# One more batch turned by a transposing DMA, and a new written order, in a fused attention and channel-mix kernel

## The chip, the core and the metric

The kernel runs on one core of a Trainium2 chip. The engines are named as in the profile: PE multiplies matrices, DVE and ACT work element by element, POOL here issues the loads, and SP issues stores and transposing DMAs. Each engine takes its own instructions strictly in order, and they wait for each other through semaphores. The metric is the device time of one execution in microseconds. A difference of 0.2% (0.4 us) is about what a measurement of this kernel can tell.

## The reference

Inputs are q, k, v of shape 8 x 8 heads x 576 tokens x 64, a scale g of 64, two mixing vectors mu_k and mu_r of 512, and weights w_k (512 x 1024), w_v (1024 x 512), w_r (512 x 512). The reference computes, for each of the eight batches:

```
kv  = k^T v                          # 64 x 64 for each head, over all tokens
u   = q kv
x   = u / sqrt(mean(u*u) + 1e-6) * g # over the 64 of a head; heads side by side: 576 x 512
xk  = mu_k * x + (1 - mu_k) * x_prev # x_prev: x of the token before, zero ahead of the first
xr  = mu_r * x + (1 - mu_r) * x_prev
out = sigmoid(xr w_r) * (relu(xk w_k)^2 w_v)
```

## The kernel before

The kernel keeps x turned (channels on partitions, tokens along the row), in two buffers xT[0] and xT[1] that alternate between batches. The work of a batch goes in stages, each a short function:

- kv (line 282) multiplies k by v; kvo copies the result out of PSUM; from the fifth batch on, kvs (line 299) writes a second copy with the halves of the partitions exchanged.
- q is turned: in the first four batches by PE (qt, line 326, copied out by qto), from the fifth on by a DMA that transposes (qd, line 303).
- u multiplies turned q by kv, in three parts. sq (line 359) squares u on ACT, red (line 363) sums the squares on DVE, and nw (line 367) is eight small DVE instructions that give the inverse root rs. mul (line 397 or 419) multiplies u by rs into y.
- y is turned into xT. There are two ways. In batches one to six PE transposes y into PSUM (x0, line 441, and x, line 450, 36 transposes together) and ACT or DVE copies it into xT multiplied by g (x0o, xo, the helper move on line 427). In batches seven and eight mul writes y into the buffer yd in another order, one DMA on SP transposes all of yd into xT (yd, line 411), and two instructions multiply xT by g in place (gx, line 415). There is one buffer yd, so each batch's mul waits for the DMA of the one before.
- wrap (line 593) fills the first token column, dif (597) takes x minus x_prev, sc (601) multiplies by mu on ACT or DVE, and add (616) adds x_prev: the result is xk (add.b.0) or xr (add.b.1).
- K (line 647) is one 128 x 288 piece of relu(xk w_k): four products on PE and an instruction on ACT or DVE that empties the bank. ks (line 639) squares it into sqk. R (line 654) is 128 tokens of sigmoid(xr w_r). V (line 662) is half of the products with w_v for 128 tokens, and fin (line 678) multiplies V by the sigmoid on DVE and stores it from SP.

The first two batches are cut finer, since their inputs and the weights are still arriving. They have words of their own: for the first batch kvc, qtc, uc, sqc, msc, rsc, mcc (lines 470 to 517; the mean of squares there is a product on PE, msc, and its inverse root on ACT, rsc), Ka and Kz (two halves of a K piece, lines 715 and 719), fu (a fused scale and add on DVE); for the second kvh, uh, sqh, redh, rsh, mulh, xh, x0h and their copies (lines 519 to 585), each for one half of the heads. Kp is a K piece and Vq a quarter of the V products in these batches. wm issues products of zeros that only keep PE busy.

What sets the order is a list written out by hand or by a search, the string ORDER (line 18): eight strings, one a period. The loop on line 795 reads it word by word and issues each word's instructions, so each engine's queue is the list with the other engines' work left out. A word is a name, its arguments (batch from 0, so batch six of this text is 5 in a word), an apostrophe where DVE and not ACT does the element work, and after "=" the PSUM banks to take, of eight. A bank is free again when the instruction that empties it has run. Loads are words as well (ld.0, ld.1, ld.2 for k, v, q), issued from POOL; yd, qd and the stores are issued from SP in the list's order.

```
for word in period.split():
    word, _, digits = word.partition("=")
    chosen[:] = map(int, digits)
    name, *args = word.rstrip("'").split(".")
    ops[name](DVE if word.endswith("'") else ACT, *map(int, args))
```

Of the kernel before, what the change touches and what calls it, by code (L numbers as in the profile page):

```python
# [19 lines left out]
    wm.2.0=1 cast.1' cast.0 kvc.0.2=23 kvco.0' qtc.0.2=45 kvco.1' wm.2.1=6 qtco.0' uc.0=7 qtco.1' uc.1=0  # L20
    qtc.2.2=12 sqc.0 msc.0=3 qtco.2' sqc.1 cols=4 msc.1=6 rsc.0 rsc.1 kvc.2.1=5 kvco.2 uc.2=1 uc.4=4 qtco.3
    mcc.0 mcc.1 difh.0.0.256.576 sc.0.0.0.256.576' sc.0.0.1.256.576' add.0.0.0.256.576 sqc.2 kvc.3.1=3 kvco.3
    msc.2=6 rsc.2 mcc.2 dih.0.2.256.576 fu.0.0.2.256.576 uc.3=5 uc.5=7 sqc.3 sqc.4 wm.2.2=2 msc.3=0 wm.2.4=3
    rsc.3 msc.4=6 mcc.3 dih.0.3.256.576 wrap.0 fu.0.0.3.256.576 wm.2.3=2 sqc.5 msc.5=1 rsc.5 Ka.0.3=3 mcc.5
    wm.1.5=0 rsc.4 mcc.4 Ka.0.2=2 Ka.0.1=5 difh.0.0.0.256 Ka.0.0=1 fu.0.0.0.0.256 Kz.0.3 Kz.0.1 sc.0.1.0
    fu.0.0.1.0.256 difh.0.1.0.256 Kz.0.2 Kz.0.0 Ka.0.7=0 Kz.0.7 fu.0.0.3.0.256 Ka.0.6=6 Kz.0.6 Ka.0.5=7
    fu.0.0.2.0.256 sc.0.1.2 sc.0.1.1' Ka.0.4=4 Kz.0.4' add.0.1.0 Kz.0.5 ksp.0.0.4.8 Kp.0.1.0'=3 Kp.0.1.1=5
    sc.0.1.3 qt.1.0=21 qto.1.0.0' kvh.0=06 kvho.0.1 Kp.0.1.3=4 kvho.0.0' qto.1.0.1' uh.2.0=7 uh.1.0=35 uh.0.0=20
    sqh.0.1.0 ksp.0.1.0.4' sqh.2.0.0 sqh.0.0.0 sqh.1.1.0 sqh.1.0.0 add.0.1.1 Kp.0.1.2=1 ksp.0.0.0.4' Vq.0.2.0=6
    Vq.0.2.1 redh.5.9.0 rsh.5.9.0 redh.0.5.0 rsh.0.5.0 mulh.0.0.0 mulh.0.1.0 Vq.0.1.0=4 Vq.0.1.1 mulh.1.0.0  # L30
    mulh.2.0.0 xh.2.2.0=12 xho.2.2.0.0 xho.2.2.0.1' qt.1.1=03 qto.1.1.0 x0h.0=72 x0ho.0.1' qto.1.1.1 Vq.0.3.0=1
    Vq.0.3.1 x0ho.0.0 kvh.1=20 kvho.1.1 ksp.0.1.4.8' mulh.1.1.0 xh.0.2.0=35 kvho.1.0' uh.2.1=7 uh.0.1=20
    xho.0.2.0.0 sqh.0.0.1 sqh.0.1.1 sqh.2.0.1 ld.0.2 xho.0.2.0.1' ld.1.2 uh.1.1=53 sqh.1.1.1 sqh.1.0.1
    redh.5.9.1 redh.0.5.1 rsh.5.9.1 mulh.0.0.1 Vq.0.1.2 Vq.0.2.2 Vq.0.3.2 rsh.0.5.1 Vq.0.1.3 mulh.1.0.1
    mulh.1.1.1 Vq.0.2.3 Vq.0.0.0=2 mulh.2.0.1 Vq.0.0.1 Vq.0.0.2 mulh.0.1.1 xh.2.2.1=53 xho.2.2.1.0 xh.0.2.1=70
    xho.2.2.1.1' xho.0.2.1.1' ld.2.2 Vq.0.0.3 dif.1.384.576 xho.0.2.1.0 sc.1.0.3.384.576' sc.1.0.1.384.576'
    sc.1.0.2.384.576' sc.1.0.0.384.576' x0h.1=35 x0ho.1.1' x0ho.1.0 wrap.1 adda.1.0.384.576 dif.1.0.384
    sc.1.0.1.0.384' tab R.0.0=0 R.0.1=7 R.0.2=3 fin.0.0
    """,
    """  # L40
    sc.1.1.0 sc.1.0.0.0.384 sc.1.0.3.0.384 fin.0.2 sc.1.0.2.0.384' Kp.1.0.0=5 Kp.1.0.2'=0 add.1.0.0.0.384
    Kp.1.0.3=7 add.1.0.1.0.384 Kp.1.0.1'=3 sc.1.1.2' sc.1.1.3' kv.2=26 Vq.0.3.3 Kp.1.1.2=0 sc.1.1.1' kvo.2.1'
    Kp.1.1.3=5 qt.2.0=73 qto.2.0.0 add.1.1.0 ksp.1.1.2.4 qt.2.1=60 ld.2.3 qto.2.0.1' qto.2.1.1' qto.2.1.0'
    kvo.2.0' Kp.1.1.0=5 Kp.1.1.1'=3 u.2.0=70 ld.1.3 ld.0.3 sq.2.0.0 sq.2.0.1 fin.0.1 Kp.1.1.4=6 add.1.1.1
    R.0.3=2 Kp.1.1.6=5 fin.0.3 u.2.2=3 sq.2.2.0 u.2.1=46 sq.2.1.1 red.2.5.9 sq.2.1.0 R.1.7=2 Kp.1.1.7=5
    red.2.0.5 nw.2.0.1 nw.2.1.2 nw.2.2.3 R.1.6=1 ld.2.4 R.1.5=2 nw.2.3.4 ld.0.4 nw.2.4.5 nw.2.5.6 nw.2.6.7
    nw.2.7.8 ksp.1.1.0.2 R.1.4=5 mul.2.1.0 Kp.1.1.5=1 R.1.8=2 mul.2.2.0 V.1.4.0=4 mul.2.1.1 x0.2=53 mul.2.0.0
    qt.3.1=16 kv.3=27 mul.2.0.1 x0o.2.0 x0o.2.1 ksp.1.0.0.8' x.2.0.4=53 V.1.6.0=0 kvo.3.1 V.1.5.0=7 ksp.1.1.6.8'
    xo.2.0.4.1' wrap.2 ksp.1.1.4.6 V.1.7.0=3 xo.2.0.4.0 dif.2 V.1.7.1 qto.3.1.0' ld.1.4 sc.2.0.1' sc.2.0.3
    sc.2.0.2' sc.2.0.0 add.2.0.1 qto.3.1.1 V.1.4.1 V.1.6.1 add.2.0.0 sc.2.1.2 fin.1.7 V.1.5.1 sc.2.1.0  # L50
    """,
    """
    K.2.3.1=5 sc.2.1.3 sc.2.1.1' K.2.2.0=1 qt.3.0=63 K.2.7.0=5 kvo.3.0' fin.1.6 K.2.6.1=2 K.2.2.1=0 qto.3.0.1'
    ld.2.5 qto.3.0.0' ld.0.5 u.3.0=31 ld.1.5 sq.3.0.1 u.3.2=6 sq.3.0.0 u.3.1=52 qd.4 add.2.1.1 sq.3.2.0 fin.1.5
    fin.1.4 K.2.1.0=0 K.2.3.0=7 add.2.1.0 K.2.0.1'=4 red.3.5.9 sq.3.1.0 sq.3.1.1 red.3.0.5 R.2.3=0 nw.3.0.1
# [12 lines left out]
    K.3.4.0'=7 nw.4.3.4 K.3.2.0=1 nw.4.4.5 nw.4.5.6 ks.3.6' nw.4.6.7 nw.4.7.8 kvs.5.0' ks.3.1 mul.4.2.0
    mul.4.1.1 mul.4.1.0 R.3.8=4 K.3.4.1=7 mul.4.0.0 V.2.3.0=1 R.3.6=4 ks.3.2 ks.3.4 mul.4.0.1 V.2.3.1 R.3.7=7
    x0.4=50 x0o.4.1' x0o.4.0 x.4.0.4=24 u.5.2=6 u.5.0=30 xo.4.0.4.0 sq.5.0.0 u.5.1=75 ld.2.7 ld.0.7 fin.2.3  # L70
    sq.5.0.1 xo.4.0.4.1' ld.1.7 V.3.6.0=1 wrap.4 sq.5.1.0 dif.4 sq.5.1.1 sq.5.2.0 R.3.5=4 V.3.6.1 qd.6 V.3.4.0=2
    sc.4.0.0 red.5.5.9 sc.4.0.1 R.3.4=4 fin.3.6 V.3.4.1 V.3.5.0=1 red.5.0.5 nw.5.0.1 sc.4.0.2 nw.5.1.2 sc.4.0.3
    V.3.5.1 fin.3.4 sc.4.1.0 add.4.0.0 add.4.0.1 nw.5.2.3 nw.5.3.4 V.3.7.0=4 fin.3.5 nw.5.4.5
    """,
    """
    K.4.1.0=2 V.3.7.1 K.4.6.0=1 K.4.5.0=2 nw.5.5.6 sc.4.1.1' nw.5.6.7 fin.3.7 K.4.0.1=4 K.4.0.0=1 sc.4.1.3'
    K.4.5.1=2 K.4.3.1=4 ks.4.0 nw.5.7.8 ks.4.5 mul.5.1.1 mul.5.0.1 K.4.1.1=5 ks.4.1 K.4.2.1=1 mul.5.0.0
    V.3.8.0=0 K.4.7.1=2 add.4.1.0 mul.5.1.0 sc.4.1.2' mul.5.2.0 x0.5=34 x0o.5.0' x.5.0.4=75 xo.5.0.4.0
    xo.5.0.4.1' kv.6=63 kvo.6.0 K.4.4.0=1 kvo.6.1' K.4.7.0=2 K.4.2.0=5 x0o.5.1' ks.4.2 kvs.6.0' kvs.6.1' wrap.5
    dif.5 K.4.3.0=3 K.4.6.1=4 ks.4.7 K.4.4.1=7 add.4.1.1 u.6.2=6 sc.5.0.1' u.6.0=12 sc.5.0.3 ks.4.3' V.3.8.1  # L80
    ks.4.6' ks.4.4 sc.5.0.0' R.4.0=5 sc.5.0.2' V.4.0.0=3 V.4.0.1 add.5.0.1 sq.6.2.0 add.5.0.0 sq.6.0.0 sq.6.0.1
    sc.5.1.3' fin.3.8
    """,
    """
    K.5.4.0=4 u.6.1=75 qd.7 sq.6.1.1 sq.6.1.0 fin.4.0 K.5.5.0=0 K.5.2.1=3 R.4.1=4 K.5.4.1=0 red.6.5.9 red.6.0.5
    nw.6.0.1 nw.6.1.2 nw.6.2.3 R.4.3=3 V.4.1.0=4 nw.6.3.4 nw.6.4.5 nw.6.5.6 nw.6.6.7 nw.6.7.8 mul.6.2.0
    K.5.0.1=0 mul.6.1.1 sc.5.1.2 V.4.3.0=3 V.4.3.1 K.5.6.0=0 K.5.1.0=6 K.5.0.0=5 mul.6.1.0 mul.6.0.1 sc.5.1.1
    kv.7=72 mul.6.0.0 kvo.7.0 sc.5.1.0' K.5.5.1=0 K.5.3.1=1 K.5.6.1'=6 K.5.2.0'=5 add.5.1.0 ks.5.2 kvo.7.1
    K.5.1.1'=7 V.4.1.1 kvs.7.1 kvs.7.0' yd.6 ks.5.1 add.5.1.1 fin.4.1 K.5.7.1=0 fin.4.3 K.5.3.0=1 ks.5.5'
    ks.5.4' K.5.7.0'=6 ks.5.3' u.7.0=52 u.7.2=7 u.7.1=04 ks.5.7' R.5.8=1 sq.7.0.0 R.5.6=3 sq.7.1.1 R.4.2=6  # L90
    gx.6.0' sq.7.0.1 V.4.2.0=1 V.4.2.1 gx.6.1' wrap.6 ks.5.0 dif.6 sq.7.1.0 sc.6.0.2 fin.4.2 R.5.4=3 R.5.5=6
# [28 lines left out]
def kernel(  # L120
# [44 lines left out]
    cols = const.tile([128, 9], FP32, name="cols")  # L165
# [228 lines left out]
    YD = (6, 7)  # L394
    yd = const.tile([128, NHP, 1 + NHP, 128], BF16, name="yd")
# [434 lines left out]
```

## Time and profile before

| what | value |
|---|---|
| median of 3 runs | 199.56 us (199.39 to 199.66) |
| the profiled execution's own time | 199.54 us |
| its span, first to last instruction | 197.8 us |
| PE busy | 188.6 us, 95% of the span |
| DVE busy | 159.3 us, 81% |
| ACT busy | 135.8 us, 69% |
| DMA traffic | HBM read 33.56 MB, written 9.44 MB |

The span is what the profile shows of the program; the execution's own time has a further 1.7 us around it. The page's first part gives each engine's busy time. The chain that ended last is followed back from the last instruction, each step to what released it. A row of the timeline gives the start, the duration of a run of equal instructions, the engine, the line of the code, what is written and read, the count, and in brackets the idle time ahead of it and what ended it. PEld is PE's loading of weights, which runs beside the products.

### The profile page before, as it was taken

To read this page: it belongs to the slowest core of one execution; us is meant where nothing else is said; L and a number is where in the kernel's file an instruction comes from. 1 tells how busy PE (TensorE), PEld (TensorE's weight loads), DVE (VectorE), ACT (ScalarE), POOL (GpSimd) and SP (SyncE) were. 2 spreads that over 40 slices of the span, in tenths; PEclk is the share of its full clock that TensorE was granted. 3 is DMA by queue.
4 is the path that set the end of the run, shared out by engine and by line. 5 is a ranking of instruction groups with operands and counts; after the bars stand their busy time and mean duration, and the time that the engine had idled before them with its cause. 6 is when DMAs were issued, how large, how long until landed. Compare 5 with 4: busy or idle time off the path is not lost.

```text
span 197.8 us, 5867 instructions
## 1 busy us (share of the span) xinstructions
PE 188.6 (95%) x2427; PEld 112.7 (57%) x2451; DVE 159.3 (81%) x348; ACT 135.8 (69%) x284; POOL 26.8 (14%) x44
## 2 busy tenths in 40 slices
PE   7989999999999999999999999999999999999991
PEld 2446844674454756477454775667454754765450
DVE  1499997996999799897999979978999969548240
ACT  3397975968876977979797799766793485637210
POOL 7763342004000400314000000000000000000000
PEclk9999999999999999999999999999999999999999
DMA  5999999999995799999999830559420654021764
GB/s 209 220 206 207 199 207 209 204 227 233 247 213 99 132 209 168 218 247 276 218 209 203 195 74 0 122 116 127 111 55 0 133 124 92 0 53 42 167 132 141
DMA packets 35950, 30.86 MB, mean 156 GB/s; under 512 B 16332, under 2 KB 30932, under 8 KB 35924
## 3 DMA queue, kind: packets, MB, share of 16 engines
q0 software_dynamic: 14912, 16.19, 48.9%
q1 hardware_dynamic: 20612, 13.77, 32.5%
q10 hardware_dynamic: 400, 0.52, 0.9%
q8 instruction: 19, 0.31, 0.6%
q14 instruction: 7, 0.06, 0.1%
HBM read 33.56 MB, written 9.44 MB: 217 GB/s over the span
## 4 chain that ended last, share of the span: by engine, by line
PE 88%; DMA 4%; issue 2%; DVE 2%; POOL 1%; ACT 1%; DVEq 0%; POOLq 0%
PE ps_v L667 29%; PE ps_km L635 29%; PE ps_r L657 16%; DMA rt<-in_v_dram 4%; PE ps_km L712 2%; PE ps_kv L291 2%; PE ps_x L439 2%; PE ps_u L320 2%; PE ps_qt L334 1%; PE ps_u L356 1%; PE ps_v L675 1%; POOL q L184 1%; PE ps_warm L265 1%; ACT sq L549 1%; DVE sqk L643 1%
## 5 line engine op out<-in xcount | busy, mean ns | idle before, releaser
L667 PE MATMUL ps_v<-wv_sb,sqk 128*128 128x512 bf16 x266 | 65.0, 379 | 1.4 <-issue 0.6
L635 PE MATMUL ps_km<-xk,wk_sb 128*128 128x288 bf16 (+3 forms) x480 | 65.0, 285 | 0.0
L635 PEld LDWEIGHTS <-wk_sb 128*128 128x128 bf16 x480 | 45.6, 98 | 16.8
L627 ACT ACTIVATE rt<-ps_km 128x288 bf16<-128x288 f32 (+3 forms) x95 | 39.2, 425 | 22.7 <-PE ps_km L635 19.5
L667 PEld LDWEIGHTS <-sqk 128*128 128x128 bf16 x280 | 26.6, 98 | 29.4 <-DVE sqk L643 0.4
L657 PE MATMUL ps_r<-wr_sb,xr 128*128 128x512 bf16 x136 | 34.9, 379 | 0.6 <-issue 0.2
L680 DVE TENSOR_TENSOR out_sb<-ps_v,sig 128x512 f32<-128x512 f32 (+1 forms) x37 | 24.2, 670 | 8.2 <-issue 3.9
L660 ACT ACTIVATE sig<-ps_r 128x512 bf16<-128x512 f32 x36 | 21.5, 601 | 12.3 <-PE ps_r L657 12.0
L605 ACT ACTIVATE m<-dx,cols 128x576 bf16<-128x576 bf16 (+1 forms) x31 | 22.5, 764 | 2.0 <-DVE dx L599 2.0
L641 ACT ACTIVATE sqk<-rt 128x576 bf16<-128x576 bf16 (+2 forms) x30 | 21.1, 717 | 1.6 <-DVE rt L629 1.5
L657 PEld LDWEIGHTS <-xr 128*128 128x128 bf16 x144 | 13.7, 98 | 14.9 <-issue 0.7
L629 DVE TENSOR_SCALAR rt<-ps_km 128x288 bf16<-128x288 f32 (+3 forms) x25 | 11.8, 477 | 9.9 <-PE ps_km L635 9.7
L365 DVE TENSOR_REDUCE ss<-sq 128x16 f32<-128x1024 bf16 (+1 forms) x12 | 15.9, 1345 | 1.0 <-ACT sq L361 1.0
L361 ACT ACTIVATE sq<-ps_u 128x512 bf16<-128x512 f32 (+1 forms) x30 | 15.2, 565 | 0.6 <-PE ps_u L356 0.3
L643 DVE TENSOR_TENSOR sqk<-rt 128x576 bf16<-128x576 bf16 (+4 forms) x27 | 13.0, 504 | 0.1
L599 DVE TENSOR_TENSOR dx<-xT 128x2304 bf16<-128x2304 bf16 (+5 forms) x13 | 11.6, 895 | 0.9 <-ACT xT L429 0.5
L622 DVE TENSOR_TENSOR xr<-m,xT 128x1152 bf16<-128x1152 bf16 x16 | 11.9, 750 | 0.0
L424 DVE TENSOR_TENSOR y<-ps_u,rs 128x512 bf16<-128x512 f32 (+1 forms) x20 | 11.4, 629 | 0.2
L622 DVE TENSOR_TENSOR xk<-m,xT 128x1152 bf16<-128x1152 bf16 (+2 forms) x16 | 10.8, 699 | 0.9 <-ACT m L605 0.6
L607 DVE TENSOR_SCALAR m<-dx,cols 128x576 bf16<-128x576 bf16 (+3 forms) x35 | 11.2, 351 | 0.1
L265 PE MATMUL ps_warm<-zeros 128*128 128x512 bf16 x22 | 8.4, 517 | 1.5 <-DVE eps L228 1.2
L429 ACT ACTIVATE xT<-ps_x,cols 128x256 bf16<-128x256 bf16 (+3 forms) x13 | 7.0, 563 | 2.9 <-PE ps_x L439 2.9
(91 smaller groups left out, 157.7 us busy)
## 6 DMA issues: line engine op xcount, KB each, us to landing
out_dram<-out_sb SPq DMA_DIRECT2D x67, 128.0 KB, 2.9
sq<-in_k_dram POOLq DMA_DIRECT2D x3, 576.0 KB, 14.5
qT<-in_v_dram POOLq DMA_DIRECT2D x3, 576.0 KB, 14.9
q<-in_q_dram POOLq DMA_DIRECT2D x3, 576.0 KB, 12.8
in_q<-in_q_dram POOLq DMA_DIRECT2D x3, 576.0 KB, 12.6
in_v<-in_v_dram POOLq DMA_DIRECT2D x3, 576.0 KB, 15.7
in_k<-in_k_dram POOLq DMA_DIRECT2D x3, 576.0 KB, 12.6
wk_sb<-in_moe_w_k_dram POOLq DMA_DIRECT2D x2, 512.0 KB, 10.3
```

What stands on the lines that cost most here:

```text
L361: ACT.activation(out=sq[:, rg(t0, n, i) if n else slice(0, 1)], in_=held["u", a, part, i][1], func=AF.Square)
L365: DVE.tensor_reduce(out=ss[:, g0:g1], in_=sq[:, g0:g1], op=ALU.add, axis=AX.X)
L605: eng.activation(out=out_, in_=in_, func=AF.Copy, scale=mu)
L622: DVE.tensor_add(out=dst, in0=m[:, hs, c0:c1], in1=x[:, hs, c0:c1])
L627: eng.activation(out=dst, in_=ps, func=AF.Relu)
L635: nc.tensor.matmul(ps[:, n, :], wk_sb[:, cc, 128 * fc:128 * fc + 128], at[b]["xk"][:, cc, c0:c1], start=(cc == 0), stop=(cc == NHP - 1))
L641: eng.activation(out=sqk[:, fcs, o:o + n], in_=src, func=AF.Square)
L643: eng.tensor_mul(out=sqk[:, fcs, o:o + n], in0=src, in1=src)
L657: nc.tensor.matmul(ps, xr[:, cc, 128 * t:128 * t + 128], wr_sb[:, cc, :], start=(cc == 0), stop=(cc == NHP - 1))
L660: ACT.activation(out=sig[b, t], in_=give("r"), func=AF.Sigmoid)
L667: nc.tensor.matmul(ps, sqk[:, fc, 128 * t:128 * t + 128], wv_sb[:, fc, :], start=(fc == 0), stop=(fc == NFC - 1))
L680: DVE.tensor_mul(out=o, in0=give(key), in1=sig[b, t][:, c])
```

## The change

Batch six (5 in the words) joins the two batches whose y is turned by a DMA: YD grows from (6, 7) to (5, 6, 7). With it x0.5, x.5, x0o.5 and xo.5 leave the list, and yd.5, gx.5.1 and gx.5.0 come into it; mul.5 writes yd instead of y, and mul.5.2.0 becomes two instructions of half the partitions. The eight periods are written anew. All other words stay, at other places: some 65 element words go from ACT to DVE and about as many from DVE to ACT, banks are numbered anew, and words move across the ends of periods. The words that warm PE up go from 12 products ahead of the list and 12 in it (one of them the list's last word) to 12 and 8. In the loads, v and k of batch three change places and k of batch four moves ahead of its q and v.

The first lines of the first period, before and after:

```
-    wm.2.0=1 cast.1' cast.0 kvc.0.2=23 kvco.0' qtc.0.2=45 kvco.1' wm.2.1=6 qtco.0' uc.0=7 qtco.1' uc.1=0
-    qtc.2.2=12 sqc.0 msc.0=3 qtco.2' sqc.1 cols=4 msc.1=6 rsc.0 rsc.1 kvc.2.1=5 kvco.2 uc.2=1 uc.4=4 qtco.3
-    mcc.0 mcc.1 difh.0.0.256.576 sc.0.0.0.256.576' sc.0.0.1.256.576' add.0.0.0.256.576 sqc.2 kvc.3.1=3 kvco.3
...
+    cast.0 cast.1' kvc.0.2=01 kvco.0' kvco.1' qtc.0.2=23 qtco.1' qtco.0 cols=4 wm.1.0=1 uc.1=5 uc.0=6 qtc.2.2=70
+    sqc.1 qtco.2' msc.1=1 sqc.0 msc.0=3 wm.1.1=7 kvc.2.1=4 rsc.0 kvco.2 rsc.1 wm.1.2=7 uc.2=2 qtco.3' uc.4=7
+    sqc.2 wm.1.3=4 kvc.3.1=0 mcc.0 kvco.3 mcc.1 difh.0.0.256.576 msc.2=3 sqc.4 uc.3=4 sc.0.0.0.256.576' uc.5=6
+    sc.0.0.1.256.576' add.0.0.0.256.576 sqc.3 msc.4=1 rsc.2 wm.1.4=0 msc.3=5 wm.3.5=0 Ka.0.0=0 mcc.2 Ka.0.2=3
...
```

Batch two, after (its first half in the first period, its second half in the second):

```
+    ksp.0.1.0.4' sqh.1.1.0 sqh.1.0.0 sqh.0.0.0 add.0.1.1 Kp.0.1.2=5 Kp.0.1.3=6 redh.0.5.0 redh.5.9.0 Vq.0.2.0=1
+    rsh.0.5.0 mulh.2.0.0 mulh.1.1.0 Vq.0.3.0=5 Vq.0.2.1 Vq.0.3.1 x0h.0=62 mulh.1.0.0 sc.0.1.1 qt.1.1=37
+    rsh.5.9.0 mulh.0.0.0 qto.1.1.1 x0ho.0.1' mulh.0.1.0 x0ho.0.0' xh.0.2.0=42 xh.2.2.0=06 xho.0.2.0.1' qto.1.1.0
...
+    sc.1.0.0.0.384 sc.1.1.0 Kp.1.0.1'=6 sc.1.0.2.0.384 Kp.1.0.2=2 Kp.1.0.3'=4 add.1.0.0.0.384 fin.0.2 sc.1.1.1'
+    R.0.0=7 sc.1.0.3.0.384' add.1.0.1.0.384 Kp.1.0.0'=6 R.0.1=4 kv.2=27 kvo.2.0 fin.0.0 Kp.1.1.2=1 sc.1.1.3'
```

Batch six, after (the end of the fourth period and the fifth):

```
+    mul.4.0.1 K.3.4.1=0 x0.4=46 x.4.0.4=73 fin.2.3 x0o.4.0' u.5.1=21 x0o.4.1 u.5.0=50 xo.4.0.4.0 sq.5.1.0
...
+    K.4.5.0=6 mul.5.0.0 mul.5.1.0 mul.5.0.1 kv.6=14 K.4.3.0'=5 K.4.0.1'=6 K.4.6.0=2 yd.5 fin.3.4 sc.4.1.3'
...
+    K.4.2.0=6 K.4.7.0=3 K.4.4.0'=2 ks.4.3' ks.4.1 ks.4.7' gx.5.1' ks.4.4 V.3.8.0=0 u.6.1=51 sq.6.1.0 u.6.2=4
+    gx.5.0' ks.4.2 u.6.0=63 sq.6.0.1 sq.6.1.1 R.4.0=7 wrap.5 sq.6.2.0 V.3.8.1 dif.5 sq.6.0.0 V.4.0.0=2 sc.5.0.2'
...
-    YD = (6, 7)
+    YD = (5, 6, 7)
```

## The prediction, made before the changed kernel ran

> **What bounds the kernel now.** I read the page first: the engines' busy shares and the chain that ended last.
>
> ```profile
> span 197.8 us, 5867 instructions
> ...
> PE 188.6 (95%) x2427; PEld 112.7 (57%) x2451; DVE 159.3 (81%) x348; ACT 135.8 (69%) x284; POOL 26.8 (14%) x44
> ...
> PEclk9999999999999999999999999999999999999999
> ...
> PE 88%; DMA 4%; issue 2%; DVE 2%; POOL 1%; ACT 1%; DVEq 0%; POOLq 0%
> ```
>
> TensorE is busy for 188.6 of 197.8 us, at full clock, and holds 88% of the chain. Next I looked where its idle time lies, stretch by stretch (PE is the first number pair).
>
> ```profile
> 25.00:38.00 13.00, 12.45 (x169) 6.07 (x171) 11.03 (x31) 9.25 (x25) 3.70 (x5) 1.00 1.22 207
> 38.00:48.00 10.00, 9.56 (x220) 6.68 (x220) 8.91 (x21) 7.46 (x15) 2.22 (x3) 1.00 1.19 229
> 48.00:193.00 145.00, 143.79 (x1700) 86.58 (x1715) 121.47 (x251) 102.31 (x212) 6.69 (x9) 1.00 0.74 138
> ```
>
> From 48 to 193 us PE idles 1.21 us in all, in gaps of 0.05 and 0.16 us put down to issue: work that PE loses there shortens the run, and nothing else can gain there. From 25 to 48 us it idles 0.99 us, with DMA loaded throughout. That is the head, where the first two batches wait for inputs and weights. Third, the timeline of the weight loads shows what paces the head:
>
> ```profile
> 15.21 0.12 PEld L712 LDWEIGHTS <-wk_sb 128*128 128x128 bf16 x2 [0.44 <-DMA wk_sb<-in_moe_w_k_dram]
> 17.75 0.52 PEld L712 LDWEIGHTS <-wk_sb 128*128 128x128 bf16 x5 [0.30 <-DMA wk_sb<-in_moe_w_k_dram]
> ```
>
> The two halves of w_k land at 15.2 and 17.7 us, and no order of instructions makes the first products earlier. The same trace has batch two's last part of v landing at 28.85 us; kvh.1, which reads it, starts at 29.17.
>
> **The change part by part.** *Transposes.* The 36 PE transposes of batch six leave:
>
> ```profile
> 114.85 0.63 PE ps_x L439 x36
> ```
>
> The chain of waits gives 0.63 us for them, inside the stretch that PE bounds: −0.63 us. [...]
>
> *Copies.* On DVE two x0o copies (0.28 and 0.27 us) and one xo (0.75) leave, on ACT one xo (1.1). Two in-place products by g come to DVE:
>
> ```profile
> L431 DVE TENSOR_SCALAR xT<-xT,cols x4: 508/512/517, 140.3 to 162.0; 128x1152 bf16<-128x1152 bf16 x4
> L413 SPq DMA_TRANSPOSE xT<-yd x2: 2957/3354/3752, 132.1 to 153.8; - x2
> DMA to landing us min/median/max: 4.9/5.3/5.7
> ```
>
> They are 2 x 0.51 us, and mul.5.2.0 becomes two halves of 0.42 instead of one of 0.41: DVE gains 0.15 us of work, ACT loses 1.1. I count nothing: PE covers it, since the sums below leave DVE slack. Without that cover it would cost 0.15, and it can gain nothing, as PE does not wait for ACT there.
>
> *The new transposing DMA.* yd.5 takes 4.9 to 5.7 us from issue to landing. It waits on SP behind the stores of fin.3.5 and delays those of fin.3.4 and qd.7, whose readers are far off. Behind it on DVE stands gx.5.1', and DVE takes instructions in order, so a late landing holds all that follows: gx.5.0, wrap.5, dif.5, sc, add.5.0, and then PE's K.5. In the new order PE has one kv (0.71 us) and 15 K words (0.49 each) between the last mul of batch six and gx.5.1', 8.06 us; from there 4 V and 4 R halves or tiles (0.86 each) and three u (0.84) to K.5.1.1, 7.75 us. The mul takes 0.68, the DMA 5.7 at most: 6.4 of 8.06 us. Cost 0; the bounds are 0 (nothing waits for less than before) and, by the slowest transpose in the trace (qT under full loads, 9.6 us on the queue instead of 3.4), 0.68 + 9.6 + 2 − 8.06 = 4.2, less the 3.3 us by which DVE's sums up to add.5.0.0 (12.5 us by rows) stay under PE's 15.81: 0.9.
>
> *Warm-up products.* 23 ahead of the end become 20; one stood behind the last product, where no store waits for it. All those gone stood before w_k's landing or where Kz.0.3 waited for DVE: 0, bounds −0.2 (wm.1.5, between Ka.0.3 and Ka.0.2) and 0.
>
> *Order: the middle and the end.* From batch three on I compared sums of rows: DVE's work from the first adda of batch two to each add.b.0, against PE's from the first Kp.1.0 to K.b. The slack was 1.5, 2.9, 3.1, 4.1, 6.4, 9.6 us for batches three to eight and becomes 1.2, 2.7, 4.7, 4.3, 7.2, 10.4. Only batch three's is thinner, and there walking DVE's queue by rows gives add.2.0.0 0.3 us ahead of K.2.1.0 (0.4 before: 62.94 against 63.36 us). The last product still ends in a half-width tile whose product and stores follow alone. Cost 0; bounds 0 (after 48 us PE has no waits to give back) and 0.4, the thinnest slack. The loads of v and k of batch three change places; kv.2 needs both. Cost 0.
>
> *Order: the head.* Here the walk does find something.
>
> ```profile
> 10.42 0.47 PE L476 MATMUL ps_kv<-rt 64*64 64x64 bf16 x18
> 10.50 1.14 DVE L516 SCALAR_TENSOR_TENSOR xT<-ps_u,cols,rs 128x384 bf16<-128x384 f32 x2 [0.28 <-ACT rs L512]
> 10.92 0.21 ACT L221 CAST kv<-ps_kv 128x64 bf16<-128x64 f32 x1
> 26.50 1.27 DVE L564 TENSOR_TENSOR y<-ps_u,rs 128x256 bf16<-128x256 f32 x4
> ```
>
> (1) ACT now runs kvco.2 ahead of rsc.1. kvco.2 waits for kvc.2.1 (to 10.89) and ends at 11.14; rsc.1 takes 0.58, so mcc.1 starts at 11.7 instead of 11.03: DVE is 0.65 late from there, and it has no rest before 25 us. (2) PE does not show it at once: ten Ka and Kz words (0.27 each) stand behind w_k's second half, which gives 17.71 + 2.7 = 20.4, and with qt.1.0, kvh.0, four Kp and three uh the first Vq comes at 25.5 (25.32 before). (3) DVE reaches redh at 25.6 (25.18 before). Then 2 x 0.70 for redh, 0.25 + 4 x 0.33 for mulh and 0.15 for a copy, with part zero now last, end at 28.8, where before part zero was through at 27.25. So xh.2.2.0 waits to 28.8. kvh.1 ends at 29.4, 0.18 earlier than before, with four Vq words done instead of six (2 x 0.43) and xh.0.2.0 (0.17) done already: 0.5 behind. (4) The second half: add.0.1.0 (0.67) now stands ahead of redh.5.9.1, xh.2.2.1 can start at 33.4 while PE is there at 33.13, and xh.0.2.1 waits 0.25 for mulh.1.1.1; against before's gaps of about 0.3 that adds 0.2. Batch two's first Kp is 0.65 late, like for like. (5) The sigmoid products R.0.0 and R.0.1 now follow three Kp words and give DVE room; of before's gaps in that stretch (0.16, 0.05, 0.23, 0.16) I let 0.3 go. Net +0.35. The bounds are −0.99, all idle time from 25 to 48 us, and +1.3, the delays of (1) and (3) to (4) added whole without the gain of (5).
>
> **Sum.** The profiled execution took 199.54 us (span 197.8 and 1.7 around it), 0.02 under the median of 199.56. 199.54 − 0.63 + 0 + 0 + 0 + 0 + 0.35 = 199.26, or 199.3 us.
>
> **The rivals.** *The head costs nothing* (or the new order fills its gaps). For it: DMA, not DVE, sets kvh.1 in both orders, and my walk adds small waits that may overlap. Against it: the 0.65 us on mcc.1 is an order written out. 199.54 − 0.63 = 198.9, and with up to half of the 0.99 us of gaps filled 198.4; I take 198.7. *The head's DVE chain decides* and the kernel is slower: place xh.2.2.0 and xh.2.2.1, price 1.3 us plus a second wait of 0.3 at K.2.1.0 whose slack is thinnest; it decides once the head costs more than 0.63. 199.54 − 0.63 + 1.6 = 200.5. For it: DVE is full from 10 to 25 us. Against it: PE can take Vq words that need nothing new. *yd.5 lands late*: gx.5.1' holds DVE, K.5 starts late as it starts 0.1 us behind add.5.0.0 even now (122.91 against 122.81 us); DMA is loaded 9 tenths until 108 us. 199.26 + 0.9 = 200.2. *The clock drops in the head*, since fewer warm-up products fill it. That it can be slow the first products show: 14 of them take 5.71 us from 1.20 on, 0.41 each, against 0.86 for four of the same width later. If that came back at 15.2 us for as long, half of some 5 us would be lost, 2.5, of which the wait for w_k's second half hides 0.5: 199.26 + 2.0 = 201.3. Against it: the row of PEclk, and the longest gap that the new order opens is 0.85 us near 7 us. [...]
>
> **How the numbers follow.** The forecast (head partly paid, PE's 0.63 kept) 0.42, own range 198.9 to 199.8; head free or better 0.22; head decides 0.25; yd.5 late 0.08; clock 0.03. The range that leaves out no more than 2 in 10 is 198.5 to 200.6. 0.2% is 0.4 us, about what a measurement of this kernel can tell. Faster: all of the second, and 0.17 of the first, 0.39. Within 0.2% (199.16 to 199.96): 0.23 of the first and 0.04 of the others, 0.27. Slower: 0.34.
>
> **What would show it.** In the changed profile: 144 instead of 180 transposes on L439 and three turnings from yd, the first landing within 6 us and DVE with no wait at gx.5.1'; mcc.1 near 11.7 us; a PE gap of over half a microsecond in front of xh.2.2.0 near 28 us; the first Kp of batch two near 37.2; PE idle from 48 us to the end no more than 1.3 us. The prediction is wrong if PE shows new waits behind DVE after 48 us, if gx.5 waits for its DMA, or if the head runs as early as before.

## The result

The forecast was 199.3 us with a range of 198.5 to 200.6. The changed kernel takes 202.26 us (median of 4 runs, 202.12 to 202.35), the kernel before 199.53 in the same comparison: a ratio of 1.0125, with a 95% interval from 1.0089 to 1.0161. It is slower, and it lies outside the range. The profiled execution of the changed kernel took 202.35 us with a span of 200.5, so the profile is of a typical execution. In the experiments below, a median takes in every execution, while the ratio beside it leaves out slow ones, over 1.5% above the kernel's fastest.

The page after, with the lines that answer to those shown of before:

```profile
span 200.5 us, 5772 instructions
...
PE 187.1 (93%) x2388; PEld 111.7 (56%) x2411; DVE 160.7 (80%) x346; ACT 137.1 (68%) x285; POOL 27.1 (14%) x44
...
PEclk9999999999999999999999999999999999999999
...
PE 82%; DMA 5%; DVE 4%; issue 3%; POOL 3%; ACT 1%; POOLq 0%
```

By these pages TensorE is busy for 1.5 us less, at full clock, but the span is 2.7 us longer. So it idles 4.2 us more. The same three stretches as before (busy time of PE is the first pair):

```profile
25.00:38.00 13.00, 12.41 (x176) 6.67 (x177) 12.26 (x33) 9.78 (x25) 3.70 (x5) 1.00 1.22 207
38.00:48.00 10.00, 9.95 (x215) 6.65 (x215) 9.30 (x21) 7.71 (x16) 1.23 (x2) 1.00 1.20 222
48.00:193.00 145.00, 140.32 (x1657) 84.22 (x1670) 121.64 (x250) 103.39 (x212) 7.68 (x11) 1.00 0.73 140
```

From 25 to 48 us PE idles 0.64 us instead of 0.99. From 48 to 193 us it idles 4.68 us, where it idled 1.21: here the time went. The list of PE's waits names what it waited for (total in us, how often, the longest):

```profile
PE ps_km L635 <- ACT rt L627: 1.7, 1, 1.7
PE ps_v L667 <- issue: 1.6, 5, 1.0
PE ps_km L712 <- DMA wk_sb<-in_moe_w_k_dram: 1.3, 2, 0.7
...
PE ps_km L635 <- PE ps_u L356: 0.7, 1, 0.7
```

Three single waits behind 48 us make 3.42 us: 1.74 in front of K.3.7.1 at 97.22 us, 1.00 in front of V.1.6.0 at 63.40, and 0.68 in front of Kp.1.1.0 at 48.95.

The rest, 1.26 us here and the 1.21 us of before, is hardly idle time. It is made of gaps of 0.05 and 0.16 us. The page before has records of 2427 products for 2451 weight loads, the page after of 2388 for 2411, so 24 and 23 products have no record. In the profiles of before_plus16 and after_again, two runs told below, none is missing, and these gaps are gone: from 48 to 193 us PE is busy for 145.00 us in the one and for 142.26 in the other, where two waits make the 2.74 us.

**The wait of 1.74 us is a chain over three engines.** The timeline of after around it:

```profile
92.95 1.49 DVE L365 TENSOR_REDUCE ss<-sq 128x20 f32<-128x1280 bf16 x1 [0.18 <-ACT sq L361]
...
93.98 0.68 ACT L641 ACTIVATE sqk<-rt 128x576 bf16<-128x576 bf16 x1
...
96.19 0.45 DVE L643 TENSOR_TENSOR sqk<-rt 128x576 bf16<-128x576 bf16 x1
...
96.76 0.41 ACT L627 ACTIVATE rt<-ps_km 128x288 bf16<-128x288 f32 x1 [2.10 <-DVE ns L384]
...
97.22 1.14 PE L635 MATMUL ps_km<-xk,wk_sb 128*128 128x288 bf16 x8 [1.74 <-ACT rt L627]
```

Read it from the end. PE starts K.3.7.1 at 97.22, when ACT has read the bank of K.3.4.0 (the ACTIVATE at 96.76). ACT had been idle for 2.10 us in front of that ACTIVATE, although the products that it reads had ended at 95.48. It waited for a place to write. rt is a ring of seven buffers (line 649), batch four has eight F chunks, and chunk 4 is the eighth in the new order. The buffer that it gets is chunk 5's, and it waits for the square that reads it, ks.3.5' on DVE: the TENSOR_TENSOR at 96.19, which ends at 96.64, 0.12 us ahead. (The trace doesn't name the buffer; that the ring is the cause is shown by the first experiment.) That square stands behind the reductions and the Newton steps of batch five. The profile names the DVE instruction that ended last (ns L384), not the one that was waited for.

**The other two waits have no partner in the trace.** The profile writes "issue" or the last instruction of PE's own:

```profile
48.95 0.82 PE L635 MATMUL ps_km<-xk,wk_sb 128*128 128x384 bf16 x4 [0.68 <-PE ps_u L356]
```

```profile
63.40 1.46 PE L667 MATMUL ps_v<-wv_sb,sqk 128*128 128x512 bf16 x6 [1.00 <-issue]
```

Everything that these words read was ready: V.1.6.0 waits for one semaphore, xo.2.0.4.0', which ended at 59.96. But counted along PE's queue (weight loads, products and semaphore instructions), the two words are instructions 1475 and 1987, and these are 512 apart. The page has a line on instruction fetches in its list of DMA queues (packets, MB, share of the engines' time):

```profile
q8 instruction: 19, 0.31, 0.6%
```

That is 19 packets of 16,384 bytes. PE's queue has 4,844 instructions, counted with the 23 products that have no record, 255 for each packet, and the two words with a wait lie 512 apart. So I take a packet to be a block of 256 instructions, with these two at the edges of blocks. The time of each packet stands in the trace's DMA records. Against the moment at which PE comes to instruction 1475 and 1987 they give this (us; worked out from the records of the runs told below):

```
                 edge 1475                                  edge 1987
                 entered  fetch began  later by  wait       entered  fetch began  later by  wait
before            47.37     45.06       2.30     0.23        64.74     59.76       4.98      -
after             48.94     46.51       2.43     0.68        63.41     61.08       2.32     1.00
after, again      48.21     45.91       2.29      -          62.68     60.36       2.32     1.00
16 more           48.58     46.35       2.23     0.41        63.05     60.78       2.28     2.51
16 fewer          49.74     46.55       3.18      -          63.15     60.43       2.72      -
before, 16 more   47.48     45.20       2.28     1.49        66.01     61.10       4.91      -
```

In these rows PE never enters a block sooner than 2.2 us after the fetch of that block began, and where it enters within 2.2 to 2.4 us it has mostly waited. The fetch itself begins 3.3 to 4.0 us after PE entered the block before, in these rows, while the loads run. By the sum of the two, 5.5 to 6.4 us, a block whose 256 instructions take PE less than about 6 us can end in a wait: an estimate. In the new order the block up to 1987 holds both qt.3 and x.2.0.4, 208 instructions in 1.4 us (57.60 to 58.99), and the whole block takes 4.9 us without its wait.

### The profile page after: what moved, and what is told of

Read it like the earlier page. It is cut to its first block, busy times and chain, and to the rows that moved or that the text cites. A ratio compares the mean times of both kernels' runs of the same rounds, so it can differ in the third digit from the quotient of the medians.

```text
span 200.5 us, 5772 instructions
## 1 busy us (share of the span) xinstructions
PE 187.1 (93%) x2388; PEld 111.7 (56%) x2411; DVE 160.7 (80%) x346; ACT 137.1 (68%) x285; POOL 27.1 (14%) x44
## 4 chain that ended last, share of the span: by engine, by line
PE 82%; DMA 5%; DVE 4%; issue 3%; POOL 3%; ACT 1%; POOLq 0%
PE ps_v L667 29%; PE ps_km L635 28%; PE ps_r L657 15%; DMA wk_sb<-in_moe_w_k_dram 5%; PE ps_kv L291 2%; PE ps_u L320 1%; PE ps_km L712 1%; PE ps_x L439 1%; PE ps_qt L334 1%; POOL rt L184 1%; PE ps_v L675 1%; PE ps_u L356 1%; POOL q L184 1%; DVE ss L365 1%; DVE ss L554 1%
## 5 line engine op out<-in xcount | busy, mean ns | idle before, releaser
L627 ACT ACTIVATE rt<-ps_km 128x288 bf16<-128x288 f32 (+3 forms) x88 | 36.3, 426 | 30.0 <-PE ps_km L635 24.8
L605 ACT ACTIVATE m<-dx,cols 128x576 bf16<-128x576 bf16 (+2 forms) x41 | 28.8, 746 | 2.4 <-DVE dx L599 2.2
L629 DVE TENSOR_SCALAR rt<-ps_km 128x288 bf16<-128x288 f32 (+2 forms) x32 | 15.1, 479 | 7.8 <-PE ps_km L635 7.4
L643 DVE TENSOR_TENSOR sqk<-rt 128x576 bf16<-128x576 bf16 (+4 forms) x32 | 15.9, 513 | 6.1 <-ACT rt L627 6.0
L641 ACT ACTIVATE sqk<-rt 128x576 bf16<-128x576 bf16 (+1 forms) x25 | 17.0, 687 | 1.7 <-DVE rt L629 1.6
L424 DVE TENSOR_TENSOR y<-ps_u,rs 128x512 bf16<-128x512 f32 (+1 forms) x15 | 8.7, 628 | 0.2
L265 PE MATMUL ps_warm<-zeros 128*128 128x512 bf16 x19 | 7.4, 528 | 1.2 <-DVE eps L228 1.2
L607 DVE TENSOR_SCALAR m<-dx,cols 128x576 bf16<-128x576 bf16 (+3 forms) x25 | 8.3, 349 | 0.2
L221 ACT COPY qT<-ps_qt 128x576 bf16<-128x576 bf16 x10 | 6.1, 643 | 3.0 <-PE ps_qt L485 2.2
## 6 DMA issues: line engine op xcount, KB each, us to landing
in_v<-in_v_dram POOLq DMA_DIRECT2D x3, 576.0 KB, 12.5
```

The lines of the kernel that those rows point to most:

```text
L605: eng.activation(out=out_, in_=in_, func=AF.Copy, scale=mu)
L627: eng.activation(out=dst, in_=ps, func=AF.Relu)
L641: eng.activation(out=sqk[:, fcs, o:o + n], in_=src, func=AF.Square)
L643: eng.tensor_mul(out=sqk[:, fcs, o:o + n], in0=src, in1=src)
```

## The experiments

**Eight buffers for rt.** Label ring8.

```
-            rts[b, fc] = work.tile([128, S], BF16, tag="rt", name="rt", bufs=7)
+            rts[b, fc] = work.tile([128, S], BF16, tag="rt", name="rt", bufs=8)
```

> The kernel after, with eight buffers instead of seven for rt (the relu of one F chunk). Theory A (buffer ring): the 1.74 us that PE idles at 97.22 us come from K.3.4.0, the eighth chunk of batch four, which is given the buffer of chunk 5 and so waits on ACT for ks.3.5' on DVE (ends 96.64); with eight buffers the wait is gone and the time falls by 1.5 to 1.75 us, to about 200.6; the waits of 0.68 at 48.95 and 1.00 at 63.40 stay. Rival B (DVE is simply behind in batch four): K.3.4.0 is freed, but the next squares and products wait for DVE instead, and less than 0.6 us comes back, 201.7 or more.

Measured: 199.89 us (199.59 to 200.46), ratio to before 0.9999 (0.9964 to 1.0035). The timeline shows no wait where 1.74 us stood:

```profile
93.97 1.03 PE L657 MATMUL ps_r<-wr_sb,xr 128*128 128x512 bf16 x4
94.83 1.63 PE L635 MATMUL ps_km<-xk,wk_sb 128*128 128x288 bf16 x12
96.30 1.03 PE L667 MATMUL ps_v<-wv_sb,sqk 128*128 128x512 bf16 x4
```

Theory A holds and rival B falls: nothing else took the wait's place. The gain is 2.4 us and not 1.75. In this execution the wait at 63.40 was absent too: the fetch began 2.41 us after the block before was entered, not 3.55. So that wait depends on when the fetch begins, and the same words in the same order show it in one execution and not in another. The step from 1.75 to 2.4 as a whole was not settled.

**Moving the edges without moving a word.** Warm-up products compute nothing that is used, and they stand ahead of everything else. Eight fewer shift all edges by 16 instructions one way (nowarm), eight more the other way (plus16).

```
-    ... wm.1.0=1 ... wm.1.1=7 ... wm.1.2=7 ... wm.1.3=4 ... wm.1.4=0 ... wm.3.5=0 ...
+    (nowarm: without these six words, eight products)
-    ... msc.3=5 wm.3.5=0 Ka.0.0=0 ...
+    ... msc.3=5 wn.8=0 wm.3.5=0 Ka.0.0=0 ...     (plus16: wn.8, eight products of 64x64)
```

> The kernel after without its eight warm-up products between the words of the first period: 16 PE instructions fewer before everything else, no other instruction moved. Theory C (instruction supply): PE's program comes in blocks of 256 instructions, the fetch of the next block starts up to 4 us after PE runs over a block's edge and ends 2.3 us later, and the waits of 0.68 us at 48.95 and 1.00 us at 63.40, which the profile puts down to issue, stand on such edges (instructions 1475 and 1987 of PE's queue, 512 apart). With 16 fewer ahead, the edge near 58 us takes in less of the dense kv, qt and x stretch: by the times of the trace of after, PE then needs 7.8 and 7.5 us from edge to edge instead of 5.7 and 4.9, over the 6.0 to 6.4 of a fetch. Both waits vanish: 1.6 us less, about 200.6. Rival D (the waits belong to the words, by DVE, ACT or a bank): they stay, 202.2. Rival E (the warm-up products keep the clock up): the head slows and the time rises, over 202.5.

> The kernel after with eight more narrow warm-up products (64 by 64, some 0.2 us in all) where PE waits for w_k near 14 us: 16 PE instructions more ahead, nothing else moved. Theory C: the block that ends at the former 63.40 us now ends inside the dense stretch; PE crosses it in 3.0 us instead of 4.9 and waits 1.0 + 1.9 = 2.9 us or more there, and the earlier one 0.9 instead of 0.7: about 2 us more in all, 204.2 (203.7 to 205). Rival D (waits tied to the words): no change, 202.2 to 202.4.

Measured: 200.55 us without the eight (199.99 to 201.4; ratio 1.0034, 0.9998 to 1.0069), 204.66 us with eight more (203.21 to 205.45; ratio 1.0216, 1.0126 to 1.0305). Of the first, PE's waits show the ring's 1.7 still there and no wait of L663 (V) any more:

```profile
PE ps_km L631 <- ACT rt L623: 1.7, 1, 1.7
...
PE ps_km L708 <- DMA wk_sb<-in_moe_w_k_dram: 1.0, 1, 1.0
```

In the second the wait in front of the products of V has grown from 1.00 to 2.51 us:

```profile
63.05 1.22 PE L673 MATMUL ps_v<-wv_sb,sqk 128*128 128x512 bf16 x3 [2.51 <-issue]
```

Theory C foretold 200.6 and 204.2. Rival D, waits that belong to the words, falls by both. The 32 instructions between the two kernels move the time by 4.1 us. Not all of that is waiting, and the number of plus16 is in part luck. Its wait grew by 1.51 us and not by 1.9, and the clock fell behind it: the granted clock is 0.50 from 63.31 to 66.73 us, which shows as the 7 in the page's row.

```profile
PEclk9999999999997999999999999999999999999999
```

Half the clock for 3.42 us loses 1.71 us, by estimate, if PE is busy throughout. This execution is the slowest of the four. Word for word against after, plus16 is 0.15 us ahead before this wait and 3.06 behind a few words later, and 1.51 + 1.71 make up that step. Of rival E little is to be seen in nowarm: the clock stays up in this profile, and the head takes 0.15 us more.

**The same in the kernel before.** Label before_plus16; the diff is wn.8 in front of wm.2.3 in before's order.

> The kernel before with the eight narrow warm-up products (16 PE instructions) added where it waits for w_k. Theory C holds for any order: before's tightest block is the one left near 47 us, with a wait of 0.23; from edge to edge PE would then need 4.5 us where the fetch takes 5.9 to 6.1, and it waits 1.4 to 1.6 us more near 46 us: 199.56 + 1.4 = 201.0 (200.5 to 201.4). If the instruction supply is not the cause: 199.6, no change.

Measured: 200.91 us (200.81 to 200.93), ratio 1.0056 (1.0039 to 1.0073). The wait is at the place and of the size foretold:

```profile
47.49 0.20 PE L362 MATMUL ps_u<-kv,qT 64*128 64x64 bf16 x2 [1.49 <-issue]
```

So before is no different in kind. Its order left 5.9 us for the block up to 1475, and its own 0.23 us at 47.37 was this same wait. The prediction has that gap among those of the head and expects DVE's order to close it.

**The changed kernel once more.** Label after_again, no diff.

> The kernel after once more, for a second profile. Are the waits of single executions or of the program? Theory A with C: of the program, 1.7 us in front of K.3.7.1 again to within 0.05, and waits in front of Kp.1.1.0 and V.1.6.0 again, of 0.3 to 1.1 us, as they depend on when a fetch gets its turn among the loads; the time 202.2. Rival: waits of about the same sum at other instructions.

Measured: 201.86 us (201.36 to 202.14), ratio 1.0102 (1.0081 to 1.0122).

```profile
PE ps_km L635 <- ACT rt L627: 1.7, 1, 1.7
...
PE ps_v L667 <- issue: 1.0, 1, 1.0
```

The buffer's 1.74 and V.1.6.0's 1.00 come back to the hundredth; the wait in front of Kp.1.1.0 is gone, against the 0.3 to 1.1 expected. There the fetch began 3.44 us after the entry of the block before, not 4.01. Here the program sets where a wait can be, the start of the fetch sets whether it is there.

**A cure by order.** Label qt_moved.

```
-    mul.2.1.0 kv.3=04 qt.3.0=21 x0o.2.1 qt.3.1=63 ... qto.3.0.1 ld.2.5 ... qto.3.0.0' ... V.1.6.1 add.2.0.0 V.1.5.1
+    mul.2.1.0 kv.3=04 x0o.2.1 qt.3.1=63 ... V.1.6.1 qt.3.0=36 qto.3.0.1 qto.3.0.0' ld.2.5 add.2.0.0 V.1.5.1
```

> The kernel after with qt.3.0 (36 transposes, 72 PE instructions in 0.3 us) and its two copies moved from the dense stretch near 58 us to behind V.1.6.1, some 5 us later. Theory C (instruction supply): PE reaches the block's edge (instruction 1987) 1.9 us later than it wanted to and finds it fetched; the wait of 1.00 us is gone, those at 48.95 and 97.22 us stay: 202.26 - 1.0 = 201.3 (201.0 to 201.6). Rival D (the wait belongs to V.1.6.0 and what it reads): it stays in front of V.1.6.0, 202.2.

Measured: 201.64 us (201.44 to 202.3), ratio 1.0102 (1.0083 to 1.0121). V.1.6.0 starts 1.16 us earlier against the words around it, so the wait is gone, as theory C says. But 0.34 us come back in front of x.2.0.4, which then stands at PE before mul.2.1.0 has ended, and qt.3.0 takes 0.74 us at its new place instead of 0.33, with a wait of 0.27 in it. At K.2.1.0 0.3 us are left of the gain. The cure was right, its price was not in my number, and the time lies 0.04 us above the 201.0 to 201.6 expected.

**The turn undone.** Label undo_turn.

```
-    K.4.6.0=2 yd.5 ... ks.4.7' gx.5.1' ks.4.4 ... u.6.2=4 gx.5.0' ...
+    K.4.5.1'=2 x0.5=41 K.4.2.1=3 x0o.5.0' x0o.5.1' ... K.4.2.0=6 x.5.0.4=05 xo.5.0.4.0 xo.5.0.4.1' ...
-    YD = (5, 6, 7)
+    YD = (6, 7)
```

> The kernel after with batch six turned by PE again and everything else in place (from V.3.8 on the banks 0 and 1 are exchanged). If the turn gives what its row says, the 36 transposes come back on PE: 202.26 + 0.63 = 202.9 (202.7 to 203.2). Rival F (the transposing DMA costs as much as it saves): 202.3 or less.

Measured: 203.64 us (203.26 to 203.93), ratio 1.0205 (1.0184 to 1.0225): 1.4 us more than after, where 0.4 to 0.9 were expected. The insertion made one wait, the bank of x0.5, which kvo.6 frees late:

```profile
PE ps_x L436 <- ACT kv L218: 0.5, 1, 0.5
```

Without it 0.9 us are left for the turn. Rival F, a turn that costs what it saves, falls for this order: the turn is worth its 0.63 or somewhat more. What the further 0.3 us are is open.

**Before's order first, the changed order from the fifth period on.** Three kernels, since the first two had faults of the seam. The first four periods are before's, with banks renamed (7 to 2, 5 to 1, 3 to 5, 6 to 4, 4 to 7, 1 to 6, 2 to 3).

```
+    (late_only: periods 1-4 of before; nw.5.5.6 V.3.7.1 nw.5.6.7 nw.5.7.8 mul.5.1.1 mul.5.2.0; periods 5-8 of after)
-    K.4.5.0=6 mul.5.0.0 mul.5.1.0 mul.5.0.1 kv.6=14 K.4.3.0'=5 K.4.0.1'=6 K.4.6.0=2 yd.5
+    K.4.5.0=6 V.3.8.0=3 V.3.8.1 mul.5.0.0 ... kv.6=14 K.4.3.0'=5 K.4.0.1'=6 fin.3.8 K.4.6.0=2 yd.5     (late_only2)
+    K.4.5.0=6 V.3.8.0=3 V.3.8.1 mul.5.0.0 ... kv.6=14 K.4.3.0'=5 K.4.0.1'=6 K.4.6.0=2 yd.5 fin.3.8     (late_only3)
```

> Before's order for the first four periods (banks renamed so that the halves fit), the changed order and the transposing DMA of batch six from the fifth period on. Theory A with C: the head's 0.33, both waits at block edges and the buffer wait all lie in the first four periods, the turn itself gives its 0.63, so 199.5 - 0.6 = 198.9 (198.6 to 199.2), faster than before. Rival F (the turn or the late order costs as well, as by a landing of 6.7 us instead of 5.7): 199.5 or more.

Measured: 200.34 us, ratio 1.0041 (1.0005 to 1.0077), where 198.9 was expected. The three waits are gone (0.19 us are left at 47.55, before's own), but kv.6 takes banks that batch six's last multiplications free:

```profile
PE ps_kv L288 <- PE ps_km L632: 0.9, 1, 0.9
PE ps_kv L288 <- DVE yd L404: 0.6, 1, 0.6
```

> As the kernel with before's order for four periods and the changed order from the fifth on, with tile 8 of batch four (V.3.8) moved ahead of batch seven's k'v. In that kernel PE idled 0.92 and 0.62 us in front of kv.6, which the seam itself made: at the seam kv.6 stands four words behind the last multiplications of batch six, whose banks it takes. V.3.8 covers it with 1.73 us of product. If the turn and the late order give their 0.63 and cost nothing: 200.34 - 1.54 = 198.8 (198.6 to 199.1), 0.7 under before. Rival F (the landing of yd.5 costs, or the late order): 199.5 or more, with a wait in front of gx.5.1 or K.5.

Measured: 200.19 us, ratio 1.0011 (0.9979 to 1.0042), where 198.8 was expected. Now DVE waits for the landing of yd.5:

```profile
122.13 0.95 DVE L427 TENSOR_SCALAR xT<-xT,cols 128x1152 bf16<-128x1152 bf16 x2 [0.91 <-DMA xT<-yd]
```

The last multiplication ended at 113.63 us, but yd.5 went out at 116.91: fin.3.8, which I had put ahead of it, had two stores in SP's queue until 116.82.

> As the second seam kernel (before's order for four periods, the changed order after), with fin.3.8 behind yd.5 instead of ahead of it. In that kernel the last multiplication of batch six ended at 113.63 us, but yd.5 was issued only at 116.91: the two stores of fin.3.8 stood ahead of it in SP's queue (114.98 to 116.82). gx.5.1' then waited 0.91 us for the landing, and K.5.1.1 started 1.25 us later against the words around it than in the kernel after. If the queue is the cause, yd.5 goes out at 113.7, nothing waits for it, and 200.19 - 1.25 = 198.9 (198.6 to 199.3) is left: the turn's 0.63 on before's order. Rival F (the turn costs as much as it saves whatever stands in the queue): 199.6 or more.

Measured: 199.38 us (198.88 to 199.96), ratio 0.998 (0.9958 to 1.0002), where 198.9 was expected. yd.5 goes out at 114.08, right behind the multiplication at 113.97, and gx.5.1' does not wait. Yet K.5.1.1 starts at 127.03, just after add.5.0.0 has ended at 126.97, and against the same words in the changed kernel PE has lost 0.8 us ahead of it. The landing is not on this path: it comes at 120.16, and gx.5.1' starts at 121.48 right behind other work. DVE's own queue paces PE here. From the end of the last multiplication to the end of add.5.0.0, 13.0 us, DVE rests for 0.5 us. In the changed kernel it nearly does so: add.5.0.0 ends at 128.98, and the first weight load of K.5.1.1 follows at 129.07. The gain on before's order is 0.2 us by the medians and 0.4 by the ratio. The interval runs from nothing to 0.8 us, so that 0.63 is neither shown nor excluded. The profile is of the slowest of the twelve executions (199.96), and how much of the rest is this path and how much the seam is left open.

**Before's head.** Label head_before: before's first two periods, after's others with eight buffers; at the seam qt.3.0, kvo.3.0 and three loads move over.

> Before's order for the first two periods (banks renamed), the changed order with eight buffers for rt from the third period on; at the seam qt.3.0, kvo.3.0 and batch six's loads move into the third period. Against the kernel with eight buffers and without warm-up products (198.55 us) it tells what the head and the first edge are worth: with the old head's 0.33 less and no 0.15 for warm-up products left out, but with before's own wait of 0.23 at the edge near 47 us: 198.55 - 0.33 - 0.15 + 0.23 = 198.3 (198.0 to 198.7). Rival G (the head costs nothing; the 0.33 read from two profiles is the spread of their inputs' landing): 198.8 or a little more, since the old head then only brings its edge wait.

Measured: 200.0 us (median), ratio 0.9987 (0.9952 to 1.0022). Seven of the ten executions go from 198.85, the profiled one, to 200.76, the other three lie above 202. The spread is too wide to tell 198.3 from 198.8, so the head's price is not shown by it.

**Both cures together.** Label ring8_nowarm is ring8 and nowarm in one.

> The kernel after with both cures: eight buffers for rt, and without its eight warm-up products in the first period. If the three waits of PE are separate, their removal adds up: 202.26 - 1.74 (buffer) - 0.68 - 1.00 (block edges) and 0.15 more in the head as in the run without warm-up products: 199.0 (198.7 to 199.4), faster than before. Rival B (one lateness behind them, DVE or ACT, that shows elsewhere once freed): not under 199.6, the better of the two single cures being at 199.9.

Measured: 198.55 us (198.0 to 199.41), ratio 0.9956 (0.9937 to 0.9975): faster than both kernels. The waits are separate and their removal adds up; the gain is even 0.3 us larger than the sum of the three, and the time a little under the 198.7 to 199.4 expected. In this profile the head did lose clock without warm-up products (the figure behind the brackets):

```profile
11.50:15.20 3.70, 3.23 (x52) 0.50 1.24 207
```

From 8.38 to 18.62 us the granted clock was 0.50. At Ka.0.5 the head was some 0.9 us behind nowarm's, whose clock stayed up. The profiled execution took 199.35 us; it and one other (199.41) had a mean granted clock of 0.971, and the four at 0.995 or more took 198.0 to 198.55. Two more variants ask which warm-up products may go; both take only 8 instructions off.

```
-    ... wm.1.4=0 msc.3=5 wm.3.5=0 Ka.0.0=0 ...
+    ... msc.3=5 Ka.0.0=0 ...                  (ring8_drop4, with eight buffers)
-    warm(12)
+    warm(8)                                   (ring8_start8, with eight buffers)
```

> The kernel after with eight buffers for rt and four warm-up products fewer: the four ahead of w_k's landing (wm.1.4, wm.3.5), 8 PE instructions. Theory C: by the times of the trace of after the two tight blocks then take 6.9 and 6.7 us from edge to edge where the slowest fetches took 6.4; both waits vanish already. The other four products stay between the first words, where the run without any showed a granted clock of 0.50 from 8 to 18 us. 202.26 - 1.74 - 1.68 = 198.8 (198.3 to 199.2); the clock in the head at 1.0 unless the inputs land late. Rival E (the products ahead of w_k matter for the clock): the clock is at 0.50 behind 15 us, 199.3 or more.

> The same number of PE instructions less as with the four products ahead of w_k gone, but taken from the twelve that run before the first input lands: eight buffers for rt, 8 instead of 12 of these. Theory C: the same edges, no waits there, 198.8 if the clock holds. Rival E' (the clock): PE then idles about 2.2 us ahead of the first k'v at 6.8 us instead of 0.6; with 2.6 us of idle time there one run showed 0.50 from 9 to 11.5 us, so the head runs at half clock in part and the time is 199.0 to 199.8, with the edges in time all the same.

Measured: 198.72 us (198.33 to 199.37), ratio 0.9933 (0.9893 to 0.9972), and 198.88 us (198.65 to 199.63), ratio 0.9942 (0.9901 to 0.9984). Eight instructions are enough. In ring8_drop4's list of PE's waits nothing is left behind the head:

```profile
PE ps_kv L472 <- DVE rt L219: 1.7, 1, 1.7
PE ps_km L708 <- DMA wk_sb<-in_moe_w_k_dram: 1.4, 2, 1.1
PE ps_warm L261 <- DVE eps L224: 1.2, 1, 1.2
```

PE enters 1475 and 1987 there 2.42 and 2.33 us after their fetches began, so it comes just in time. In the other, with four products fewer at the start, the granted clock falls in the head as rival E' said, at almost no cost (0.1 us behind after's head from 20 us on):

```profile
7.00:9.00 2.00, 1.75 (x79) 0.82 1.21 206
9.00:11.50 2.50, 2.50 (x61) 0.50 1.21 203
11.50:15.20 3.70, 3.66 (x47) 0.97 1.24 207
```

## Why the prediction was wrong, step by step

*Transposes, −0.63: right.* The profile has 144 transposes on L439 and three turnings. Undoing the turn cost 1.4 us, 0.9 without the wait that the insertion made.

```profile
L439 PE MATMUL ps_x<-ident,y x144: 186/190/200, 27.6 to 102.4; 64*128 64x64 bf16 x144
```

*Copies and warm-up products, 0: not contradicted.* DVE's total grew by 1.4 us, and no wait of PE goes back to the copies. The warm-up product that stood behind the last tile moves the end of PE's work by some 0.2 us but, as forecast, not the time, since no store waits for it.

*The new transposing DMA, 0: right in the sum, wrong in its margin.* yd.5 landed after 6.7 us and not within 6; the slowest had been 5.7 before:

```profile
DMA to landing us min/median/max: 6.7/6.7/6.7
```

It landed at 122.06, and gx.5.1' started at 122.99 behind other work of DVE, with no wait. But of the 3.3 us that I gave DVE up to add.5.0.0, 0.09 us were left. PE's 15.81 us held: it took 15.90 from kv.6 to K.5.1.1. I had let both queues start at the last multiplication, though, and kv.6 had started 1.92 us ahead of its end (113.39 against 115.31); and from there DVE took 13.67 us and not 12.5. late_only3 shows the same path at its limit.

*Order: the head, +0.35: about right by subtraction, not shown by itself.* The last product that is stored ends 3.01 us later than before (196.11 against 193.10). The three waits add 3.42; the transposes and before's own wait at 47.37 take off 0.63 and 0.23; 0.45 remain for the head and all else. The second profile gives 0.41 in the same way. My steps within it were rougher. mcc.1 started at 11.44, foretold for 11.7, and DVE had a rest of 0.70 us at 16.5 to 17.2, where I had said it had none. xh.2.2.0 started at 28.69 (28.8), but not behind one gap of half a microsecond: the delay went into smaller waits. Batch two's first Kp started at 37.59 (37.2), behind R.0.2 that had moved ahead of it.

*Order: the middle and the end, cost 0 with bounds of 0 and 0.4: this step failed.* It cost 3.42 us in the first profile and 2.74 in the second. I had compared DVE's sums with PE's up to the inputs of each batch's K words, and those sums held: no K word waited for its x. What I left out were two other resources. One is the ring of seven rt buffers, which ties the evacuation of an eighth chunk on ACT to a square on DVE; I had not followed ACT's queue at all behind the head. The other is PE's own instruction supply, for which I had no row in mind, though the page lists the queue and before's trace has the gap, at 47.37 us. The bounds of 0 and 0.4 thus left out the only two costs that came. I also read the gaps of 0.05 and 0.16 us behind 48 us as idle time with an unknown cause. They are products without a record; that nothing could be gained there was right all the same.

*The rivals.* None of them was the cause. "The head's DVE chain decides" put 0.3 us at K.2.1.0; no wait is there. "yd.5 lands late" did not happen in this kernel. "The clock drops in the head" did not happen in its two profiles either. It did in others, at a price of 0.1 us in ring8_start8 and some 0.9 in ring8_nowarm, not the 2.0 that I had set.

With the ring and the edges cured and everything else as changed, the kernel takes 198.7 us. The other terms of the forecast, with before's own edge wait, give 199.54 − 0.63 + 0.35 − 0.23 = 199.0. The 0.3 us between the two are not traced.

## What to carry to other kernels

When an order is written anew, follow every ring of buffers across it: note for each allocation which earlier reader frees its buffer, on which engine, and what stands ahead of that reader. Count instructions as well as microseconds on the engine that bounds: mark every 256th instruction of its queue, the block that the packets here suggest, and keep more time between two marks than the next block needs to come under the loads of that stage (here some 6 us from 40 to 62 us, an estimate from up to 4.0 us ahead of a fetch and 2.2 to 2.4 from its start). A gap that the profile puts down to "issue" on the bounding engine is a question, not a floor. Here the small ones were products without a record and the large ones fetches. Compare the count of products with that of weight loads first; then adding or taking away a few idle instructions ahead of it is a cheap test of what it is.

## What was unexpected in the hardware

PE's fetches of 16 KB came too late in these kernels: PE waited for them for 0.19 (late_only) to 2.51 us (plus16). From 40 to 62 us, with a DMA share of 1.19 in after, a fetch began 2.4 to 4.0 us after PE had entered the block before, and where PE then waited, it could enter the block 2.2 to 2.4 us after that. Behind 100 us, with a DMA share of 0.48, the eight fetches of after began from 4.2 us ahead of that entry to 0.8 us behind it, and no wait for instructions follows them. The DMA share alone doesn't set this: from 20 to 36 us, at a share of 1.22, those of after began 0.8 to 1.6 us behind the entry. What starts a fetch is left open. Sixteen instructions more or less ahead of it all changed the time by −1.7 and +2.4 us, a part of the latter by the clock (1.7 us in the profiled execution).

PE's granted clock fell to 0.50 after rests of 2.46 us (ring8_start8, ahead of the first k'v), 2.63 (ring8, whose inputs landed late) and 2.51 (plus16, the wait for instructions), in undo_turn (mean granted clock 0.992) after 1.76, and in ring8_nowarm from 8.38 us on, where PE idled for 1.06 us between 4 and 7 us and for 1.00 between 7 and 9. It stayed at 1.00 after 1.74 in ring8_drop4 and in after. The falls lasted 3.41 or 3.42 us, in ring8_nowarm 10.24, three times that. What starts and ends a fall is not shown. What a fall cost here depended on what waited behind it: in ring8_start8 the fall took the place of the wait for w_k, 1.4 us in ring8_drop4 (198.88 us against 198.72 there with the clock up), in plus16, where 1.71 us were lost, nothing did.

Executions of the same head differ by more than the head's price. The first k'v of the kernels with after's order and all warm-up products started, by its first weight load, between 6.80 and 8.54 us in six profiles, and the first Ka between 15.14 and 16.27. A term of 0.3 us in this head can't be read from two profiles.
